# A forward and backward pass in one kernel: the last wq product in one piece, and seven zero stores in other places

## The chip, the cores and the metric

The kernel runs on one core of a Trainium2 chip. The metric is the time of one execution on the device in microseconds, as the median of several runs. A core has engines that run side by side and wait for each other through semaphores: TensorE (PE in the profile, with its weight loads as PEld), VectorE (DVE), ScalarE (ACT), GpSimd (POOL) and SyncE (SP), which here does little but issue transfers (DMAs). Data lies in HBM; the engines work on SBUF (128 partitions), and TensorE writes to PSUM, from where VectorE or ScalarE must copy a result before it can be stored ("eviction").

## The reference

One token goes through four layers that use the same weights: attention (A1), MLP (B2), attention (A3), MLP (B4), each on the layer norm of its input and added to it. Then all gradients are computed.

```
# attention: 32 query heads, 4 key heads, the last W=4096 of 32768 cached positions
q = x @ wq;  p = softmax(q k^T * Dh**-0.5);  out = (p v) @ wo
# MLP: D=1024, F=3584
h = x @ w1 + b1;  act = h * tanh(softplus(h));  out = act @ w2
# forward
x = x + A(layernorm(x)); x = x + B(layernorm(x)); x = x + A(layernorm(x)); x = x + B(layernorm(x))
out, vjp = jax.vjp(f, x, k_cache, v_cache, wq, wo, w1, b1, w2);  return out, *vjp(grad_out)
```

With one token every product is a matrix by a vector, and every weight's gradient is an outer product of two vectors, summed over the two layers that share the weight. The gradients of the key and value caches have the caches' full length: the 28672 positions ahead of the window are zero, and must be stored as zeros, 512 KB at a time in 112 pieces.

## The kernel before

All instructions are written out in the order in which each engine runs them; nothing is reordered. SP's order is thus the order of the calls in the source, and a transfer that stands behind another in it is issued behind it. There are eight semaphore lanes for SP's transfers, so a transfer is issued only when the eighth before it has landed.

**Weights.** wq, K, V and wo are loaded at the start. w1 and w2 do not fit beside them and are streamed through rings of buffers: `queue` lists the loads in order, and `rel(ring, i)`, called when a buffer has been used, lets `pump()` issue the next load into it (lines 157 to 212). A load is therefore issued when an older piece is done with, some pieces ahead of its own use.

**The chain.** Forward: `attn_fwd` A1, `mlp_B2_fwd`, `attn_fwd` A3, `mlp_B4` (B4's forward and backward in one, in four blocks of w1), then `attn_bwd` for A3, `mlp_B2_bwd`, and `attn_bwd` for A1. The two w2 passes (`w2_pass`, line 598) go over 14 pieces ("chunks") of w2: for each, four products with the activations, eight transposes that ScalarE evicts, a multiply-and-reduce on VectorE (`ttr`), and in the next step eight small products that free the buffer (`pairs`). In B2's backward pass a w1 pass follows, with 16 half rows of w1 in the same manner (line 851). Every stage needs the one before it, so a load that comes late delays everything behind it.

**The zero stores.** `zeros(n)` (line 140) issues the next n stores of zeros on SP at the place in the order where it is called. The calls are spread over the chain: `Z_` in `w2_pass` (a map from the chunk to a count, called behind that chunk's `rel`), `ZB4` behind each block of B4, `Z_` in `attn_fwd` and `attn_bwd` (three and more places each), a map in the w1 pass (line 849), and single calls. The source is a zeroed part of SBUF (`zlo`, `zt`, at the end `z8`).

**The gradients of the weights.** During the last `attn_bwd` (A1), `out_step` starts the jobs that form the gradients: step 0 stores eight zeros, steps 1 and 2 turn rows, and steps 3 to 6 run jobs (`run_jobs`). A dW2 job (`pair_half`) is four outer products on TensorE into four PSUM banks and four evictions by VectorE and ScalarE (`ev_out`, which gives each eviction to the engine with the smaller sum of costs so far); every second one issues two stores of 512 KB out of one of seven stage buffers each. The order of the jobs is 14 dW2 jobs, then dW1 jobs alternating with jobs for dK and dV (four stores of 512 KB after every fourth), then four groups of four 512-KB stores of dWo and two 1-MB stores of dWq.

Step 3 is called when dq of A1 is there; then comes the last product with wq (64 matmuls in `attn_bwd`, line 805), which gives the gradient of the input x, a small output that no other stage needs. Between eighths of this product (`h % 4 == 3`) step 4 runs one job. Every second dW2 job has a third argument of 1 in `add`, by which `run_jobs` issues one zero store behind it.

Of the kernel before, what the change touches and what calls it, by code (L numbers as in the profile page):

```python
# [21 lines left out]
def kernel(  # L22
# [283 lines left out]
    gpair = kt([P, 4, TD], BF16, "gpair")  # L306
# [329 lines left out]
    def mlp_B2_fwd(x_col):  # L636
        zeros(4)
        sv, n_bf, g0 = ln_fwd(x_col, "B2")
        hacc = one_tile("acc", TF)
        for i in range(16):  # L640
            t, hf = i // 2, i % 2
            w, ring, sl = take(("w1h", i))
            for b in range(NW2):
                fb = hf * NW2 + b
                o = (b // 2) * 2 * P + b % 2
                mm(hacc[:, fb:fb + 1], w[:, o:o + 2 * P - 1:2], n_bf[:, t:t + 1], i == 0 and b == 0, t == TD - 1)
            rel(ring, sl)
            if i == 1:
                bcast_g(gpair[:, LI["B4"], :])
        zeros(2)  # L650
        h = wk("h", TF)
        nc.vector.tensor_add(h[:], hacc[:], b1_f[:])
        dact = kt([P, TF], FP32, "dact_B2")
        mish(h[:], apair[:, 1, :], dact[:], TF)
        sv["dact"] = dact
        R, dps, ds = w2_pass(apair[:, 1, :], gpair[:, LI["B4"], :], {8: 1, 9: 1, 10: 1, 11: 1})
        nc.gpsimd.memset(sA, 0.0)
        zsrc[:] = [zt, 2048]
        da4 = kt([P, TF], FP32, "da4")
        y = d_cols(R)  # L660
        x_new = kt([P, TD], FP32, "x_B2")
        nc.vector.tensor_add(x_new[:], x_col[:], y[:])
        da_merge(da4[:], dps, ds)
        return x_new, sv, da4
# [84 lines left out]
    def attn_bwd(g_col, g_bf, l, sv, last, nxt, F_, Z_, step):  # L749
        fill_kind("wo")  # L750
        big = two_banks()
        for d in range(TD):
            for n in range(8):
                mm(big[n // 4][32 * (n % 4):32 * (n % 4) + 32, :].rearrange("p (h x) -> p h x", h=4),
                   bc(g_bf[:, d:d + 1]), wo[:, 4 * n:4 * n + 4, d * P:(d + 1) * P], d == 0, d == TD - 1, tile_position=(0, 32 * (n % 4)))
        if last:
            p_t, ds_t = sB, wo[:, 1, :]
            wo_dead()
            nc.gpsimd.dma_start(wo[:, 0, :], p3_d[:])
        else:  # L760
            p_t, ds_t = sv["p"], sA
        zeros(Z_[0])
        acc = one_tile("acc", HQ)
        j_cols(big, acc, 8, F_[0], True)
        do32 = wk("do32", HQ)
        nc.vector.tensor_copy(pad[:, :, 0:8], acc[:].rearrange("p (g h) -> p g h", g=G))
        nc.vector.tensor_copy(do32[:], acc[:])
        pr = jkf[:, 0:P]
        nc.vector.tensor_mul(pr[:].rearrange("p (c h) -> p c h", c=NC), do32[:, None, :].to_broadcast([P, NC, HQ]),
                             sv["o32"][:, None, :].to_broadcast([P, NC, HQ]))  # L770
        nc.gpsimd.tensor_copy(dos[:, LI[l], :], do32[:])
        step(0)
        fill(F_[1])
        fill_kind("V")
        big = two_banks()
        scores(big, Vf, False)
        sps = sm_tile(P, 1)
        mm(sps[:], pr[:], one[:], True, True)
        sd = wk("sd", 1)
        nc.vector.tensor_copy(sd[:], sps[:])  # L780
        zeros(Z_[1])
        for h in range(2):
            nc.vector.scalar_tensor_tensor(out=ds_t[:, h * 512:(h + 1) * 512], in0=big[h][:], scalar=sd[:, 0:1],
                                           in1=p_t[:, h * 512:(h + 1) * 512], op0=ALU.subtract, op1=ALU.mult)
        sv["p"], sv["ds"] = p_t, ds_t
        if not last:
            nc.gpsimd.dma_start(p3_d[:], sB)
            nc.gpsimd.dma_start(sB, p1_d[:])
            sv["p"] = wo[:, 0, :]
        step(1)  # L790
        fill(F_[2])
        to_keys(ds_t)
        fill_kind("K")
        qacc = one_tile("acc", HQ)
        step(2)
        keys_mm(K[:], fold, qacc, F_[3])
        if not last:
            rings["rb"] += [7, 1, 2, 3, 4, 5, 6]
            pump()
        nc.scalar.activation(dqpair[:, LI[l], :], qacc[:], ACT.Copy, scale=scale)  # L800
        zeros(Z_[2])
        step(3)
        fill_kind("wq")
        R = one_tile("R", 512)
        for h in range(HQ):
            for hf in range(2):
                g = 2 * hf + h % 2
                mm(R[32 * g:32 * g + 32, :].rearrange("p (t d) -> p t d", t=4), bc(dqpair[:, LI[l], h:h + 1]),
                   wq[:, 4 * hf:4 * hf + 4, h * P:(h + 1) * P], h < 2, h >= HQ - 2, tile_position=(0, 32 * g))
            if h % 4 == 3 and h < 31:  # L810
                step(4)
        y = d_cols(R, hook=lambda: step(5))
        tt = wk("xx", 2 * TD)
        nc.vector.tensor_copy(tt[:, 0:TD], y[:])
        return ln_bwd(tt, sv, g_col, nxt, hook=lambda: step(6))

    def mlp_B2_bwd(g_col, g_bf, sv, x3):
        bcast_g(g_bf)
        R, dps, ds = w2_pass(apair[:, 0, :], g_bf, {10: 1})
        zeros(3)  # L820
        dh = kt([P, TF], FP32, "dh_B2")
        da_merge(dh[:], dps, ds, sv["dact"][:])
        nc.vector.tensor_copy(hpair[:, 1, :], dh[:])
        y = d_cols(R)
        x4_bf = kt([P, TD], BF16, "x4_bf")
        nc.vector.tensor_add(x4_bf[:], x3[:], y[:])

        NT, NV = 4, 3
        dhb = [kpf, jk[:]]
        for hf in range(2):  # L830
            for v in range(2):
                ncb = 2 if v == 0 else 1
                ps = ptile(FP32, "dhp")
                for i in range(ncb):
                    for tt in range(2):
                        col = hf * NW2 + 2 * (NT + 2 * v + i) + tt
                        mm(ps[:, i * 256 + tt:i * 256 + tt + 255:2], bc(hpair[:, 1, col:col + 1], P), ident_bf[:], i == 0 and tt == 0, True)
                evac(dhb[hf][:, v * 512:v * 512 + ncb * 256], ps[:, 0:ncb * 256], ncb * 256, "DA"[(hf + v) % 2])
        nacc = one_tile("acc", TD)
        nv = wk("nv", 16)  # L840
        pend = []

        def pairs(i, w, ring, sl):
            t, hf = i // 2, i % 2
            for k in range(8):
                fb = hf * NW2 + k
                mm(nacc[:, t:t + 1], w[:, k * P:(k + 1) * P], hpair[:, 1, fb:fb + 1], i == 0 and k == 0, hf == 1 and k == 7)
            rel(ring, sl)
            zeros({9: 2, 12: 1, 14: 1}.get(i, 0))

        for i in range(16):
            w, ring, sl = take(("w1h", i))
            T8([w[:, (k // 2) * 256 + k % 2:(k // 2) * 256 + k % 2 + 255:2] for k in range(8)], w[:, 0:1024], "A")
            ttr(w[:, 1024:1792], dhb[i % 2][:, 0:768], nv[:, i:i + 1])
            if pend:
                pairs(*pend.pop())
            pend.append((i, w, ring, sl))
        pairs(*pend.pop())
        tt = wk("xx", 2 * TD)
        n3 = nv[:].rearrange("p (t h) -> p t h", h=2)  # L860
        t3 = wk("t3", TD)
        nc.vector.tensor_add(t3[:], n3[:, :, 0], n3[:, :, 1])
        nc.vector.tensor_add(tt[:, 0:TD], t3[:], nacc[:])
        sv["dh"] = dh
        return ln_bwd(tt, sv, g_col, "A1"), x4_bf
# [168 lines left out]
    def wo_dead():  # L1034
# [42 lines left out]

        for n in range(NW2 // 2):
            add("w2a", n, lambda c=2 * n: pair_half(row_sp["w2"], c, w2_out, w2_lhs, 0))
            add("w2", n, lambda c=2 * n: pair_half(row_sp["w2"], c, w2_out, w2_lhs, 1), 1)  # L1080
        for n in range(16):
            add("w1", n, lambda t=n // 2, hf=n % 2: w1_job(t, hf))
            add("kv", n, lambda n=n: kv_step(n))
# [26 lines left out]
    def out_step(i):  # L1110
        if i == 0:
            nc.scalar.copy(z8.bitcast(FP32), zlo[:, 0:2].bitcast(FP32).to_broadcast([P, 2048]))
            zsrc[:] = [z8, 4096]
            zeros(8)
        elif i < 3:
            rows_turn(row_sp["w2"], i - 1, w2_sp[i - 1], "rep")
        elif i > 2:
            run_jobs(1 if i == 4 else 2)

    ZB4 = [12, 11, 9, 7]  # L1120
    FT4 = [(0, 0, 0, 0), (10, 2, 2, 2), (10, 2, 2, 2), (10, 2)]
    FB4 = [(1, 0), (1, 0), (1, 0), (1, 2)]

# [3 lines left out]
    x3, sA3 = attn_fwd(x2, "A3", False, sB, [3, 2, 8, 2, 2, 2], [8, 4, 17])  # L1127
    tt, sB4 = mlp_B4(x3, da4)
    g3, g3b, _ = ln_bwd(tt, sB4, gcol, "A3", nfill=2)
    g2, g2b, _ = attn_bwd(g3, g3b, "A3", sA3, False, "B2", [4, 3, 5, 2], [3, 1, 3], lambda i: None)  # L1130
    (g1, g1b, _), x4_bf = mlp_B2_bwd(g2, g2b, sB2, x3)
    zeros(4)
    g0, g0b, _ = attn_bwd(g1, g1b, "A1", sA1, True, "X0", [0] * 4, [0, 0, 0], out_step)
# [39 lines left out]
```

## Time and profile before

| what | value |
|---|---|
| median of 3 runs | 432.07 us (430.75 to 433.14) |
| profiled execution | 431.02 us, span from first to last instruction 429.2 us |
| bytes moved | 170.5 MB (70.8 read, 99.1 written), mean 397 GB/s |
| busy share | PE 75%, VectorE 55%, ScalarE 51%, GpSimd 4% |
| mean granted clock of TensorE | 0.757 |
| zero stores of 512 KB out of `misc` | 97, median 10.2 us from issue to landing |
| eviction in a job, ScalarE / VectorE | 629 / 599 ns |

The busy time of an engine does not tell whether it bounds the kernel: TensorE's matmuls overlap, and a share is an average over stages. The DMA row of the page is near full throughout; the rate beside it in GB/s tells where the transfers queue and where there are gaps. In the lists of instructions, "[0.64 <-DMA K<-in_B_w_dram]" means that the engine sat idle for 0.64 us and that a load into K from a weight of B ended it. The tile names are those of the buffers: loads of w2 and w1 in the backward pass go into K, those of the forward pass into wo and misc; a store "out_dram<-misc" is one of zeros.

### The profile page before, as it was taken

The page shows a single profiled execution, that of the slowest core. Times are in us where ns is not written, and L with a number is a line of the kernel's source. Part 1 is how long each engine was busy: PE and PEld are TensorE (multiplying, and loading weights), DVE is VectorE, ACT ScalarE, POOL GpSimd, SP SyncE. Part 2 cuts the span into 40 slices and gives each one's busy share as a digit, 9 for nine tenths or more (in the row PEclk, how much of TensorE's full clock was granted, in tenths as well). Part 3 has the DMA queues.
Part 4 walks back from the last instruction along what each step waited for, and adds up shares of the span by engine and source line. Part 5 has one row for each costly group of instructions (what it writes and reads, how often), then busy time and mean ns, then how long its engine had stood idle before and what let it go on. Part 6 is the DMA issues. An engine that isn't in the chain of part 4 may idle for free.

```text
span 429.2 us, 9216 instructions
## 1 busy us (share of the span) xinstructions
PE 321.2 (75%) x3732; PEld 188.3 (44%) x3732; DVE 234.4 (55%) x532; ACT 219.1 (51%) x335; POOL 15.4 (4%) x54
## 2 busy tenths in 40 slices
PE   3476736367697898878788898887799799999830
PEld 1154315345455587756646565764423223321100
DVE  2035102068535346555537288673367998899940
ACT  1036101036436356646534267482487699999940
POOL 2000000000000000000000000000400111000000
PEclk9999555569889979999989989685955555555555
DMA  8999999999999999999999999999999999999995
GB/s 329 423 419 419 411 408 399 406 407 378 387 418 409 417 417 365 417 409 384 381 408 406 350 397 386 373 362 421 411 421 417 419 413 413 403 409 412 410 413 242
DMA packets 49975, 170.50 MB, mean 397 GB/s; under 512 B 4848, under 2 KB 5900, under 8 KB 45836
## 3 DMA queue, kind: packets, MB, share of 16 engines
q1 hardware_dynamic: 49456, 168.84, 99.2%
q0 software_dynamic: 416, 1.06, 0.7%
q8 instruction: 29, 0.48, 0.4%
q14 instruction: 14, 0.11, 0.1%
q10 hardware_dynamic: 60, 0.01, 0.0%
HBM read 70.79 MB, written 99.10 MB: 396 GB/s over the span
## 4 chain that ended last, share of the span: by engine, by line
DMA 40%; PE 35%; ACT 11%; DVE 7%; issue 3%; SPq 0%; ACTq 0%; DVEq 0%
DMA K<-in_B_w_dram 9%; DMA wo<-in_A_wo_dram 8%; PE tp L264 8%; PE R L244 7%; DMA out_dram<-misc 7%; DMA K<-in_A_k_cache_dram 5%; DMA wo<-in_B_w_dram 4%; PE sm L244 4%; PE acc L244 4%; ACT wo L899 4%; PE op L244 3%; ACT K L237 3%; PE lo L244 3%; DMA out_dram<-wo 3%; ACT wq L899 3%
## 5 line engine op out<-in xcount | busy, mean ns | idle before, releaser
L237 ACT COPY K<-tp 128x1024 bf16<-128x1024 bf16 x60 | 58.8, 1016 | 14.3 <-PE tp L264 13.3
L264 PE MATMUL tp<-ident_bf,K 128*128 128x128 bf16 x656 | 52.0, 238 | 6.4 <-ACT K L237 2.8
L244 PE MATMUL op<-wo 2*128 2x512 bf16 (+2 forms) x123 | 52.1, 562 | 5.0 <-ACT wo L899 2.7
L244 PEld LDWEIGHTS <-wo 128*128 128x128 bf16 (+2 forms) x590 | 24.4, 101 | 61.8 <-issue 53.5
L264 PEld LDWEIGHTS <-K 128*128 128x128 bf16 x656 | 44.3, 109 | 12.7 <-issue 9.6
L237 ACT COPY wo<-tp 128x1024 bf16<-128x1024 bf16 x33 | 33.5, 1023 | 25.7 <-PE tp L264 22.9
L899 ACT CAST wo<-op 128x512 bf16<-128x512 f32 (+1 forms) x51 | 31.2, 629 | 7.9 <-DMA out_dram<-wo 1.8
L596 DVE CUSTOM_DVE_ANT_0 K<-K,kp 128x1024 bf16<-128x1024 bf16 (+1 forms) x22 | 24.6, 1127 | 2.8 <-PE R L244 1.0
L235 DVE COPY jk<-R 128x512 f32<-128x512 f32 (+1 forms) x11 | 7.3, 665 | 33.9 <-PE R L244 33.9
L264 PE MATMUL tp<-ident_bf,wo 128*128 128x128 bf16 x336 | 24.4, 226 | 0.6 <-ACT wo L237 0.5
L244 PE MATMUL acc<-wo 2*128 2x512 bf16 (+1 forms) x41 | 24.3, 593 | 0.2 <-DVE V L896 0.2
L244 PE MATMUL hi<-wo 2*128 2x512 bf16 x41 | 24.3, 592 | 0.0
L244 PE MATMUL lo<-wo 2*128 2x512 bf16 x41 | 24.1, 587 | 0.0
L264 PEld LDWEIGHTS <-wo 128*128 128x128 bf16 x336 | 20.1, 101 | 6.9 <-issue 6.8
L237 ACT CAST jk<-hi 128x512 bf16<-128x512 f32 x4 | 2.6, 661 | 37.7 <-PE hi L244 37.7
L244 PE MATMUL sm<-wo 2*128 2x512 bf16 (+1 forms) x33 | 19.8, 600 | 1.3 <-DVE cols L384 1.3
L896 DVE CAST wo<-op 128x512 bf16<-128x512 f32 (+1 forms) x32 | 18.4, 599 | 4.1 <-PE tp L930 1.5
L235 DVE CAST jk<-lo 128x512 bf16<-128x512 f32 x4 | 2.8, 711 | 31.9 <-PE lo L244 31.9
L235 DVE COPY K<-tp 128x1024 bf16<-128x1024 bf16 x22 | 14.9, 690 | 9.6 <-PE tp L264 9.5
L244 PE MATMUL R<-wo 2*128 2x512 bf16 (+1 forms) x33 | 19.6, 593 | 0.6 <-DVE wo L896 0.4
L237 ACT COPY wq<-tp 128x1024 bf16<-128x1024 bf16 x13 | 13.0, 1018 | 11.7 <-PE tp L264 8.8
L364 ACT ACTIVATE cols<-cols,eps_t 128x1 f32<-128x1 f32 x4 | 1.2, 294 | 33.4 <-DVE cols L361 33.4
(293 smaller groups left out, 656.2 us busy)
## 6 DMA issues: line engine op xcount, KB each, us to landing
out_dram<-misc SPq DMA_DIRECT2D x97, 512.0 KB, 10.2
out_dram<-wo SPq DMA_DIRECT2D x39, 512.0 KB, 9.4
K<-in_B_w_dram SPq DMA_DIRECT2D x28, 512.0 KB, 8.1
K<-in_A_k_cache_dram SPq DMA_DIRECT2D x9, 1024.0 KB, 14.9
wq<-in_A_wq_dram SPq DMA_DIRECT2D x8, 1024.0 KB, 10.0
out_dram<-wq SPq DMA_DIRECT2D x8, 1024.0 KB, 13.5
K<-in_B_w_dram SPq DMA_DIRECT2D x16, 448.0 KB, 6.1
out_dram<-wo SPq DMA_DIRECT2D x16, 448.0 KB, 7.2
```

Of the source, the lines that this page charges most:

```text
L235: return nc.vector.tensor_copy(out_ap, in_ap)
L237: return nc.scalar.copy(out_ap, in_ap)
L244: return nc.tensor.matmul(out_ap, lhsT=lhsT, rhs=rhs, start=start, stop=stop, skip_group_check=True, **kw)
L264: nc.tensor.transpose(ps[:, b * P:(b + 1) * P], ap, ident_bf[:])
L364: nc.scalar.activation(lnv[:], var[:], ACT.Ln, bias=eps_t[:, 0:1], scale=1.0)
L596: return nc.vector.tensor_tensor_reduce(out=w, in0=w, in1=vec, scale=1.0, scalar=0.0, op0=ALU.mult, op1=ALU.add, accum_out=acc_col)
L896: nc.vector.tensor_copy(out_ap, in_ap)
L899: nc.scalar.copy(out_ap, in_ap)
```

## The change

The product with wq in the last `attn_bwd` is no longer interrupted: step 4 is not called, and the jobs that ran in it follow behind the product, in the same order. dW2's jobs no longer issue zero stores. The seven stores go to other calls: one behind chunk 2 in the w2 pass of B2's forward pass, two behind dq in A3's backward pass (3 becomes 5), one behind chunk 1 and two at the end of the w2 pass of B2's backward pass (3 becomes 5), and one behind step 4 of the w1 pass. In addition one store moves from block 0 of B4 to block 2. The `attn_bwd` of A3 never ran jobs in step 4, so its product is as before.

```diff
 # mlp_B2_fwd
-        R, dps, ds = w2_pass(apair[:, 1, :], gpair[:, LI["B4"], :], {8: 1, 9: 1, 10: 1, 11: 1})
+        R, dps, ds = w2_pass(apair[:, 1, :], gpair[:, LI["B4"], :], {2: 1, 8: 1, 9: 1, 10: 1, 11: 1})
 # attn_bwd, in the loop over heads of the wq product
-            if h % 4 == 3 and h < 31:
-                step(4)
 # mlp_B2_bwd
-        R, dps, ds = w2_pass(apair[:, 0, :], g_bf, {10: 1})
-        zeros(3)
+        R, dps, ds = w2_pass(apair[:, 0, :], g_bf, {1: 1, 10: 1})
+        zeros(5)
 # the w1 pass
-            zeros({9: 2, 12: 1, 14: 1}.get(i, 0))
+            zeros({4: 1, 9: 2, 12: 1, 14: 1}.get(i, 0))
 # the list of jobs
-            add("w2", n, lambda c=2 * n: pair_half(row_sp["w2"], c, w2_out, w2_lhs, 1), 1)
+            add("w2", n, lambda c=2 * n: pair_half(row_sp["w2"], c, w2_out, w2_lhs, 1))
 # out_step
-            run_jobs(1 if i == 4 else 2)
-
-    ZB4 = [12, 11, 9, 7]
+            run_jobs(2)
+
+    ZB4 = [11, 11, 10, 7]
-    g2, g2b, _ = attn_bwd(g3, g3b, "A3", sA3, False, "B2", [4, 3, 5, 2], [3, 1, 3], lambda i: None)
+    g2, g2b, _ = attn_bwd(g3, g3b, "A3", sA3, False, "B2", [4, 3, 5, 2], [3, 1, 5], lambda i: None)
```

## The prediction

> **What bounds the kernel now.** I read the page's slices first, then the windows of 5 us, then the timeline around the loads, then the waits of the store queue. The slices (columns: busy tenths, granted clock, GB/s in 40 slices of 10.7 us):
>
> ```profile
> PEclk9999555569889979999989989685955555555555
> DMA  8999999999999999999999999999999999999995
> GB/s 329 423 419 419 411 408 399 406 407 378 387 418 409 417 417 365 417 409 384 381 408 406 350 397 386 373 362 421 411 421 417 419 413 413 403 409 412 410 413 242
> ```
>
> The DMA row says that transfers are always under way, but the rate says more: 418 GB/s where stores queue (155 to 160 us), and holes to 350. A 512-KB zero store at 418 GB/s costs 0.524 MB / 0.418 = 1.25 us. That is the price of each moved store wherever the transfers queue; in a hole it is free. So the question is which it meets. Windows (columns: engines' busy us and counts, clock, DMA share, GB/s):
>
> ```profile
> 220.00:225.00 5.00, 4.84 (x63) 2.15 (x63) 1.27 (x5) 1.01 (x1) 0.00 (x0) 0.66 1.02 394
> 240.00:245.00 5.00, 4.20 (x73) 2.08 (x70) 0.69 (x1) 1.03 (x2) 0.00 (x0) 1.00 0.92 331
> 275.00:280.00 5.00, 4.10 (x80) 3.23 (x79) 5.00 (x13) 5.00 (x6) 0.00 (x0) 0.98 0.98 343
> 280.00:285.00 5.00, 4.30 (x80) 3.28 (x78) 4.30 (x10) 4.91 (x6) 0.00 (x0) 1.00 0.98 348
> 310.00:315.00 5.00, 4.67 (x40) 1.63 (x40) 3.17 (x5) 3.72 (x8) 0.00 (x0) 0.78 1.02 431
> 315.00:320.00 5.00, 5.00 (x44) 1.40 (x40) 3.13 (x5) 3.65 (x7) 0.00 (x0) 0.50 1.01 418
> 320.00:325.00 5.00, 5.00 (x40) 1.47 (x36) 2.72 (x5) 4.21 (x7) 0.00 (x0) 0.50 1.03 415
> 325.00:330.00 5.00, 4.75 (x29) 2.35 (x25) 3.66 (x6) 3.71 (x7) 0.00 (x0) 0.50 1.03 417
> 330.00:335.00 5.00, 3.26 (x19) 1.25 (x22) 4.57 (x17) 3.13 (x6) 0.00 (x0) 0.50 1.03 419
> 415.00:420.00 5.00, 0.00 (x0) 0.00 (x0) 0.00 (x0) 0.00 (x0) 0.00 (x0) 0.50 1.03 415
> ```
>
> From 310 us the transfers are full; the last eviction ends at 413 and stores drain to 428. Ahead of that, the chain waits for weights that queue behind zero stores:
>
> ```profile
> 188.23 0.40 PE L244 MATMUL lo<-K,npair 128*32 128x512 bf16 x4 [2.84 <-DMA K<-in_B_w_dram]
> ...
> 243.85 2.98 SPq L149 DMA_DIRECT2D out_dram<-misc  x3
> 251.72 9.33 SPq L182 DMA_DIRECT2D K<-in_B_w_dram  x8
> 258.25 0.40 PE L244 MATMUL R<-K,apair 128*32 128x512 bf16 x4 [0.64 <-DMA K<-in_B_w_dram]
> ...
> 276.20 8.08 SPq L182 DMA_DIRECT2D K<-in_B_w_dram  x9
> 286.09 1.04 PE L264 MATMUL tp<-ident_bf,K 128*128 128x128 bf16 x8 [1.18 <-DMA K<-in_B_w_dram]
> ```
>
> And the end is not simply a full queue: between 340 and 381 us SP, which issues the stores, itself waits for evictions (us in total, times, longest):
>
> ```profile
> SPq L1002 <- ACT wo L899: 6.5, 8, 1.2
> SPq L1002 <- DVE wo L896: 3.2, 3, 1.4
> SPq L1002 <- ACT K L899: 2.8, 3, 1.2
> ```
>
> The waits of that stretch sum to 19.5 of 41 us, while the evicting engines wait for a store only once there (0.8 us). So dW1, dK and dV run at the pace of the evictions, and only the last block (dWo and dWq) is bound by transfers: its first store is issued at 381.73 and lands 6.7 us later; 15 more stores of 1.25 us and 8 of 2.5 us are 38.8 us, and the last lands at 428.2, 39.8 us on.
>
> **The change, part by part.** Seven stores, 8.8 us of transfers, leave the dW2 jobs; bytes and instructions stay. A step counts as far as it moves 381.73 (the first dWo store) or the drain behind it.
>
> *One zero in the first w2 pass (after chunk 2).* From 100 to 110 us every chunk's first product starts within 0.05 us of its load's landing, at a pitch of 1.25 us: saturated. The new store stands in SP's queue ahead of chunk 9's load, so chunks 9 to 12 come 1.25 later; chunk 13's load is limited by its own issue (104.75 to 110.4) and gives 0.7 back, until the loads of 160 us, which start right behind a run of zeros, take it up again. Bounds 0 and +1.25; I take +1.1, near the upper end, since the pitch is that of a full queue.
>
> *One zero from B4's block 0 to block 2.* Block 2's loads queue behind block 0's zeros: 8.1 us from issue to landing, where block 1's, behind fewer, took 5.6, and PE idles 2.84 us for them (188.23). One store less gives -1.25 (bounds -1.25 and 0). In block 2 it delays only K loads not needed until 236, and fills the hole of 238 to 244 us (311 GB/s). Taken: -1.25.
>
> *Two zeros behind dq in A3's backward pass, one after chunk 1 of the second w2 pass.* SP issues the two at some 247.7 and 249, ahead of chunk 7's load (251.72, landing at 258.2, 6.5 us). The transfers run at 363 to 418 GB/s in between, 0.4 us short of full, so chunk 7 comes 2.1 to 2.5 later, and it has no slack (0.64 wait above). Chunk 1's store is ahead of chunk 9's load: another 1.25. From chunk 7 on the pitch is 1.28, the transfers' own, and VectorE's 1.15 to 1.23 a chunk wins nothing back. Bounds +2.3 (hole and deeper queue help) and +3.75; taken +3.5.
>
> *Zeros 3 to 5 behind that pass, one after step 4 of the w1 pass.* The hole at 276 to 278 (268 GB/s) holds 0.9 us and step 7 has 0.25 slack, so 2.5 become 1.4. From step 7 the loads set the pace at 1.1 each; step 4's store adds 1.25, but the slow stretch from 280 to 288 (352 GB/s, 1.3 us under full) may take it in. Bounds +1.5 and +3.75; taken +2.2.
>
> Together the chain reaches the last attention's backward pass 5.55 later.
>
> *The product in one piece.* Before, 8 heads' worth ran between jobs. From the first evictions (311.3) to the last dW2 store (336.9) VectorE and ScalarE are idle 6.5 and 5.6 us (25 us less the busy sums of the five rows from 310, 17.25 and 18.42, less the 1.3 and 1.0 ahead of the first), mean 6.0; two waits for stage buffers (329.4 and 333.3, some 1 us each) are in it and go with the seven zeros. After, the first pair's evictions end at 314.2 and the engines sit until the product, begun at 312.4, is through. The nearest row is the product of the same 64 matmuls at 220.72: its first half ran at half clock, the rest at full (0.66 in the row), 5.1 us; the wq product at 240.18 took 3.6 at full clock; all at half would be 16 groups of 0.427 = 6.8. With 5.1 it ends at 317.5, the idle is 3.7, and 1.5 of other waits (the 1.3 that PE waits for the layer norm's columns among them) stay: 5.2, so -0.8; the stage wait of 376 goes too: -1.3 in sum. With 3.6 it is -2.9; with 6.8 and no gain at 376, +1.7.
>
> Here the Trainium skill has a rule: in "TensorE: Matmul & The Clock Gate", Part 1, the half clock is the default and about 3.4 us of busy array lift it. By it an unbroken product would lift the clock where the chopped one did not, the 5.1 case; without it, at 0.5 as in the rows from 315 on, the 6.8 case, which puts the sum 1.7 to 2.5 us higher. The row at 220 agrees with the rule: half clock for 3.4 us, then full.
>
> *The relief of the drain.* With no zeros queued, the first dWo store still stands behind four dK stores that kv's last job releases together at 377.2: an unqueued load takes 4.3 (issue of 276.20), so 377.2 + 4.3 + 4 x 1.25 = 386.5 against 388.4: -2.0 at most. With stores of dW1 still queued, -0.5. Taken -1.8. The 39.8 us behind it do not change: that is why 8.8 us less to store gains 2.
>
> POOL issues the same work; SP issues no more transfers than before, and its order is otherwise kept.
>
> **Sum.** +1.1 -1.25 +3.5 +2.2 -1.3 -1.8 = +2.45 us. The profiled execution took 431.0 (span 429.2 and 1.8 around it), so 433.5; the median of the three runs shown, 432.07, is 1.05 above it, so I predict 434.5. Ends added: -2.35 and +9.95.
>
> **Rivals.**
> (a) *The drain bounds everything from 310 us on.* For it: 409 to 431 GB/s in all rows. Against: SP's 19.5 us of waits for evictions. Were the evictions able to run ahead, the end would move by the chain less all seven stores: +5.55 - 8.75 = -3.2, so 427.8, or 428.9 by the median. It decides where the first dWo store is issued no later than its old place (381) although the chain comes 5.5 later; from 384 on the end is not earlier than before (384 + 4.3 = 388.3).
> (b) *The holes take the stores in.* Losses against 418 GB/s between 245 and 291 us sum to some 4 us; if all are filled, the two backward terms are 3.4 in place of 5.7, and with 0 for the first pass the sum is near -1: 431. Against: the pace there is set by landings.
> (c) *Everything is paid and the product stays at half clock*: +1.25 -1.25 +3.75 +3.3 +1.7 -1 = +7.75: 439.8.
>
> **How the numbers follow.** Forecast (shift of +0.5 to +5) 0.50, (c) 0.20, (b) 0.14, (a) 0.16. About 0.5% (2.2 us) is what a measurement of this kernel can tell. Faster: (a) and a little of (b), 0.18. Same: the rest of (b) and 0.12 of the forecast, 0.24. Slower: 0.58. Range: 429.5 (all but most of (a)) to 440.5 (with (c)); the forecast's own is 432.5 to 437.
>
> **What will show it.** In the profile after: chunk 7 of the second w2 pass some 2.5 us further behind the pass's start and chunk 13 3.5; PE's wait for B4's block 2 shortened to 1.6; step 7 of the w1 pass waiting for its load by over 1 us; the 64 matmuls unbroken and 5 us long; the first dWo store at some 386 and the last landing 45 us behind it. I am wrong if the w2 pass keeps its length, if the rate between 315 and 345 stays at 415 with no hole, or if the drain behind the first dWo store is shorter than 44 us.

## The result, and the profile after

The changed kernel takes 437.19 us (median of 4 runs, 435.93 to 438.11), the kernel before 432.31 us beside it (4 runs, 430.75 to 433.14). The ratio is 1.0099, with a 95% interval of 1.0073 to 1.0125: slower by 4.3 us (3.2 to 5.4), or 4.9 by the medians. The prediction was +2.45.

The profiled execution of the changed kernel took 437.84 us, with a span of 436.1. It is 0.65 us above its median, while the profiled execution of before (431.02) was 1.3 below its own. The two traces thus show 6.9 us between the spans, 2.0 to 2.6 more than the runs do. This matters below.

The three slice rows of the page after:

```profile
PEclk9999555569799889989989895875886555555555
DMA  8999999999999999998999999999998979999997
GB/s 330 424 420 417 411 408 402 408 407 404 406 414 408 417 408 387 387 385 308 369 415 406 396 398 370 359 409 421 408 426 329 368 302 404 386 374 411 408 412 319
```

Two kinds of gap are seen. One is new: slices 30 to 32 (329, 368, 302 GB/s, about 327 to 360 us), where the seven stores no longer stand behind the dW2 jobs. The other lies earlier and is not new: slice 18 (308, 196 to 207 us), deeper than before (384), and slices 24 and 25 (370 and 359, 262 to 284 us), where before had 373 and 362 one slice later. The windows of 5 us of the changed kernel (columns as before: busy us and counts of PE, PEld, DVE, ACT, POOL, then clock, DMA share, GB/s):

```profile
240.00:245.00 5.00, 4.26 (x75) 2.13 (x74) 0.72 (x2) 1.21 (x2) 0.00 (x0) 1.00 1.04 389
...
320.00:325.00 5.00, 4.67 (x48) 2.33 (x52) 1.89 (x3) 2.74 (x6) 0.00 (x0) 0.80 1.01 425
...
330.00:335.00 5.00, 4.32 (x27) 2.72 (x27) 3.68 (x9) 3.00 (x6) 0.00 (x0) 0.50 0.71 287
335.00:340.00 5.00, 4.41 (x26) 1.50 (x24) 4.63 (x13) 5.00 (x10) 0.00 (x0) 0.50 0.70 279
...
350.00:355.00 5.00, 4.54 (x30) 1.49 (x30) 4.53 (x11) 3.50 (x9) 3.00 (x11) 0.50 0.63 242
```

At 330 to 340 us VectorE and ScalarE are busy 60 to 100% of the time while the transfers run at 280 GB/s; 10 us earlier, in the same part of the work, before had 415 and 417. (The window of 240 to 245 us, 331 before, now has 389: more is in flight there, none of it for chunk 7.) In the new gap the evictions set the pace: the store queue waits for them in 27.2 of the 33 us from 327 to 360.

The time is lost ahead of that. This is the timeline around the loads of the second w2 pass, changed kernel (start, duration or stretch, engine, line; in brackets the idle time and what ended it):

```profile
246.81 5.93 SPq L149 DMA_DIRECT2D out_dram<-misc  x5
...
253.32 1.78 SPq L182 DMA_DIRECT2D K<-in_B_w_dram  x2
...
255.76 0.55 SPq L149 DMA_DIRECT2D out_dram<-misc  x1
...
257.24 8.57 SPq L182 DMA_DIRECT2D K<-in_B_w_dram  x5
...
263.64 0.62 PE L244 MATMUL R<-K,apair 128*32 128x512 bf16 x4 [5.70 <-DMA K<-in_B_w_dram]
...
276.50 2.82 SPq L149 DMA_DIRECT2D out_dram<-misc  x5
...
282.74 4.41 SPq L182 DMA_DIRECT2D K<-in_B_w_dram  x5
...
290.40 1.03 PE L264 MATMUL tp<-ident_bf,K 128*128 128x128 bf16 x8 [2.96 <-DMA K<-in_B_w_dram]
```

Five zero stores now stand ahead of chunk 7's load, and TensorE waits 5.70 us for that chunk where it waited 0.64. Five more stand ahead of the w1 pass's step 7, and it waits 2.96. The chain that ended last goes by loads a little behind these two. Its longest pieces in this stretch are the load of chunk 9, issued behind one more zero store (257.24, landed at 267.47); the fourth of the five stores ahead of the w1 pass (278.07); and the load of step 12, issued when that store had landed (288.42):

```profile
257.24 10.23 DMA K<-in_B_w_dram
...
278.07 10.27 DMA out_dram<-misc
...
288.42 8.86 DMA K<-in_B_w_dram
```

29 of the 40 us from 257 to 297 us are loads and a zero store; before had no zero store among the long pieces there. At chunk 7 VectorE is 5.6 us later than before (258.69 to 264.30; 0.7 of it is there when the pass starts), at the last attention's backward pass 10.0 (300.90 to 310.90), and at 380.41 us of before still 9.1.

The wait for chunk 7 has a sequel. These are the windows behind it, first of the changed kernel, then of before:

```profile
265.00:270.00 5.00, 4.60 (x58) 3.18 (x56) 3.12 (x7) 2.84 (x3) 0.00 (x0) 0.50 1.00 385
...
260.00:265.00 5.00, 4.64 (x82) 3.22 (x81) 4.86 (x8) 3.93 (x5) 0.00 (x0) 1.00 0.99 380
```

In the changed kernel TensorE's granted clock is half from 261.55 us for 10.24 us, and the products of chunks 7 to 11 follow each other at 1.7 us (2.2 where chunk 9's load ends a wait of 0.40), against 1.27 at full clock before. The loads of chunks 10 and 11 landed at 268.74 and 269.98, ahead of their products at 269.23 and 270.93, so there TensorE and not the transfers sets the pace. From chunk 7 to chunk 13 this kernel takes 10.0 us, before 7.6.

The product in the timeline of the changed kernel (start, duration):

```profile
322.38 5.32 PE L244 MATMUL R<-wq,dqpair 128*32 128x512 bf16 x64
```

The 64 matmuls run unbroken. The end of the drain, in the DMA issues of the changed kernel: the first dWo store, issued at 390.30, and the last dWq store, issued at 422.00 (size, us from issue to landing):

```profile
out_dram<-wo SPq DMA_DIRECT2D x1, 512.0 KB, 4.4
...
out_dram<-wq SPq DMA_DIRECT2D x1, 1024.0 KB, 13.0
```

The first dWo store is issued 8.6 us later than before (381.73), but lands in 4.4 us instead of 6.7, with little queued ahead of it. The waits of the store queue for evictions from 350 to 391 us add up to 26.9 of 41 us, against 19.5 of 41 from 340 to 381 us of before; the two longest rows (us in total, times, longest):

```profile
SPq L1000 <- DVE wo L894: 12.0, 8, 3.0
SPq L1000 <- ACT wo L897: 5.4, 7, 1.1
```

### The profile page after: what moved, and what is told of

Its sections match the earlier page's. It is cut to its first block, busy times and chain, and to the rows that moved or that the text cites. A ratio compares the mean times of both kernels' runs of the same rounds, so it can differ in the third digit from the quotient of the medians.

```text
span 436.1 us, 9207 instructions
## 1 busy us (share of the span) xinstructions
PE 323.6 (74%) x3732; PEld 192.6 (44%) x3732; DVE 233.7 (54%) x532; ACT 218.3 (50%) x335; POOL 15.4 (4%) x54
## 4 chain that ended last, share of the span: by engine, by line
PE 25%; ACT 10%; DMA 8%; DVE 5%; issue 2%; SPq 0%; ACTq 0%; DVEq 0%
DMA K<-in_B_w_dram 6%; ACT wo L897 5%; PE R L244 5%; PE tp L264 5%; PE op L244 4%; PE acc L244 3%; PE sm L244 3%; ACT wq L897 3%; PE lo L244 2%; DMA out_dram<-misc 2%; PE hi L244 2%; ACT K L237 2%; PE tp L928 1%; DVE wo L894 1%; DVE jk L235 1%
## 5 line engine op out<-in xcount | busy, mean ns | idle before, releaser
L264 PE MATMUL tp<-ident_bf,K 128*128 128x128 bf16 x656 | 55.2, 247 | 8.7 <-DMA K<-in_B_w_dram 3.8
L264 PEld LDWEIGHTS <-K 128*128 128x128 bf16 x656 | 46.8, 113 | 16.0 <-issue 10.6
L244 PE MATMUL hi<-wo 2*128 2x512 bf16 x40 | 23.1, 579 | 0.0
L244 PE MATMUL sm<-wo 2*128 2x512 bf16 (+1 forms) x36 | 21.6, 600 | 0.0
L244 PE MATMUL R<-wo 2*128 2x512 bf16 (+1 forms) x36 | 21.4, 593 | 0.0
L235 DVE COPY wo<-tp 128x1024 bf16<-128x1024 bf16 x19 | 12.8, 689 | 10.2 <-PE tp L264 10.1
L244 PEld LDWEIGHTS <-npair 128*32 128x32 bf16 x184 | 6.2, 116 | 26.0 <-issue 22.6
```

The source lines that it names most:

```text
L235: return nc.vector.tensor_copy(out_ap, in_ap)
L244: return nc.tensor.matmul(out_ap, lhsT=lhsT, rhs=rhs, start=start, stop=stop, skip_group_check=True, **kw)
L264: nc.tensor.transpose(ps[:, b * P:(b + 1) * P], ap, ident_bf[:])
```

## The experiments

Three theories stood after the result. **T1**: the seven stores are paid by the chain, because they queue ahead of loads for which it waits, and the tail gives back only a little. **T2**: the product in one piece, or the gaps in the drain, cost the end. **T3**: the store taken from block 0 of B4 is the surprise. The trace after has 248 GB/s at 200 to 205 us where before had 321, and more transfers are in flight ahead of the second w2 pass, so a queue that ran dry at 202 us would be paid for at 258. Rival (a) of the prediction, the drain as the bound from 310 us on, is tested as well.

Ratios are to runs of the kernel before on the same chip, whose medians were 432.2 to 432.9. One thousandth is 0.43 us, and prices below are ratios times 432.3.

### The product alone

```diff
-            if h % 4 == 3 and h < 31:
-                step(4)
 ...
-            run_jobs(1 if i == 4 else 2)
+            run_jobs(2)
```

> The product alone in one piece, the seven zero stores left in the dW2 jobs. T1 (the seven stores ahead of the loads cost the chain 10 us, the product gives 0.9 back): nothing moves ahead of 310 us, the 64 matmuls take 5.1 to 5.4 us, and the time is 0.5 to 1.5 us under the kernel before (431 by its median of 432.3). T2 (the engines that evict stand still behind the unbroken product, the store queue runs dry, and that costs the end): 2 to 4 us over it, 434.5 to 436.5, with slices under 350 GB/s between 312 and 325 us.

Measured: 432.20 us (12 runs), ratio 0.9989 (0.9971 to 1.0007): -0.5 us, not told apart from nothing. T2 falls for the product. The product takes 5.32 us as in the changed kernel, and in this run, with the seven stores behind the jobs, the transfers never let go. Windows of this kernel:

```profile
325.00:330.00 5.00, 4.41 (x24) 1.39 (x24) 4.48 (x10) 5.00 (x10) 0.00 (x0) 0.50 1.03 419
330.00:335.00 5.00, 3.08 (x19) 0.81 (x18) 4.26 (x12) 4.18 (x9) 0.00 (x0) 0.50 1.03 419
```

Its first dWo store among the DMA issues:

```profile
out_dram<-wo SPq DMA_DIRECT2D x1, 512.0 KB, 6.7
```

The evictions behind the product come up to 5.4 us later than before at 314 us, 2.1 later at 328 and on time at 336; at 380 us they are 0.9 later again. What the pause holds up, the next 20 us make good, and the first dWo store still takes 6.7 us to land.

### The seven stores alone

```diff
-w2_pass(apair[:, 1, :], gpair[:, LI["B4"], :], {8: 1, 9: 1, 10: 1, 11: 1})
+w2_pass(apair[:, 1, :], gpair[:, LI["B4"], :], {2: 1, 8: 1, 9: 1, 10: 1, 11: 1})
 ...
-        R, dps, ds = w2_pass(apair[:, 0, :], g_bf, {10: 1})
-        zeros(3)
+        R, dps, ds = w2_pass(apair[:, 0, :], g_bf, {1: 1, 10: 1})
+        zeros(5)
 ...  (w1 pass, A3's backward pass, ZB4 and the jobs as in the change)
```

> All seven stores moved as in the change (block 0 of B4 to block 2 too), the product still in eighths between the jobs. T1: the chain comes to the last attention's backward pass 10 us later, as in the changed kernel, and the time is that of the changed kernel plus 0.9 lost with the product: 437.5 to 438.5 (5 to 6 over before). T2: the stores cost only what the drain doesn't give back, and without the unbroken product the time is within 2 us of before, 431 to 434.

Measured: 437.54 us (6 runs), ratio 1.0105 (1.0084 to 1.0126): +4.5 us, as T1 had it. That is the whole loss of the change; the product's share in it is -0.3 (1.0099 against 1.0105), less than the runs tell apart. VectorE is 11.4 us later at 300.9 us and 9.9 at 380.

### The seven stores left out, with and without the product in one piece

```diff
         job, f, z = jobs.pop(0)
         f()
-        zeros(z)
+        del zero_jobs[:z]
```

> The product in one piece, and the seven stores of the dW2 jobs left out altogether: 3.7 MB of the zeros of the cache gradients are never written. The chain is that of the kernel before, the tail that of the changed kernel, 10 us earlier. T1: only product (-0.9) and relief (-2.2) are seen: 3.1 us under before, 429. Rival (a), the transfers bound everything from 310 us on: all seven stores are gained, 8.75 us, 423.5. T2: no gain or a loss, 432 to 435.

> The seven stores of the dW2 jobs left out altogether (3.7 MB of the cache gradients' zeros are never written), the product in eighths as before. T1: the relief of the drain alone, 2.2 us under before, 430; the difference to the run with the product in one piece is the product's 0.9. Rival (a): 8.75 us under before, 423.5.

Measured: with the product in one piece 429.15 us, ratio 0.9917 (0.9888 to 0.9945), -3.6 us; with it in eighths 429.95 us, ratio 0.9928 (0.9910 to 0.9947), -3.1 us; T1 had 429 and 430. Rival (a) falls: 8.75 us of transfers vanish and 3.1 us are gained. T2 falls for the gaps as well: they are there (below), and the time is lower. The product is worth another -0.5, again within the interval. What the tail looks like without the seven (product in eighths), in windows:

```profile
325.00:330.00 5.00, 4.75 (x30) 0.81 (x28) 4.04 (x7) 3.96 (x8) 0.00 (x0) 0.50 0.98 399
330.00:335.00 5.00, 4.64 (x24) 2.81 (x24) 4.26 (x13) 3.20 (x7) 0.00 (x0) 0.50 0.79 316
335.00:340.00 5.00, 3.78 (x22) 0.65 (x19) 4.79 (x16) 3.71 (x8) 0.00 (x0) 0.50 0.71 286
...
345.00:350.00 5.00, 4.84 (x27) 1.19 (x26) 4.83 (x11) 5.00 (x12) 0.93 (x6) 0.50 0.78 305
```

And its first dWo store, issued at 381.94, among the DMA issues:

```profile
out_dram<-wo SPq DMA_DIRECT2D x1, 512.0 KB, 4.3
```

The dWo store is issued when it was before (381.73) and lands 2.2 us sooner (386.28 for 388.47). Between 330 and 350 us the transfers have room that no eviction fills.

The run with all seven moved and this one have the same tail, the product in eighths and no store behind a job, and differ in the chain alone. So the seven stores, with the move in B4, cost the chain 1.0105 - 0.9928 = 0.0177, or 7.6 us (+-1.2), for 8.75 us of transfers.

### The move in B4, taken back and alone

```diff
-    ZB4 = [12, 11, 9, 7]
+    ZB4 = [11, 11, 10, 7]
```

> The changed kernel with block 0 and block 2 of B4 left at 12 and 9 zero stores. T1 with the prediction's price of that move (-1.25 in the chain): 438.5, 1.3 over the changed kernel's 437.2. T3 (a store less in block 0 lets the store queue run dry near 202 us, and the bytes not moved there come back ahead of the second w2 pass): the stretch from 200 to 210 us is back at 320 to 370 GB/s, chunk 7 of that pass comes 2.5 to 3 us sooner than in the changed kernel, and the time is 434 to 435.5.

> The kernel before with one zero store moved from block 0 of B4 to block 2, and nothing else. T1 with the prediction's price: -1.25, so 431. T3: 200 to 210 us falls to 250 to 300 GB/s, the loads of the second w2 pass land 2.5 to 3 us later, and the time is 434.5 to 435.5.

Measured: the changed kernel without this move 437.58 us, ratio 1.0106 (1.0072 to 1.0141), as the changed kernel; the move alone 431.95 us, ratio 1.0006 (0.9985 to 1.0027). So it is worth +0.3 us (+-0.9): neither the -1.25 of the prediction nor T3's +2.5 to +3. T3 falls, and the gap that it started from is not the move's doing: the same stretch has 178 GB/s in the run with the seven stores left out, and 174 in the one with the product alone, where nothing was changed ahead of it. The window of the first of these:

```profile
200.00:205.00 5.00, 4.26 (x78) 3.44 (x76) 2.10 (x4) 2.88 (x3) 0.00 (x0) 1.00 0.51 178
```

Why the -1.25 did not come is seen in TensorE's waits for blocks 2 and 3 with the move alone:

```profile
186.41 0.40 PE L244 MATMUL lo<-K,npair 128*32 128x512 bf16 x4
...
187.75 0.40 PE L244 MATMUL lo<-K,npair 128*32 128x512 bf16 x4
...
190.18 0.40 PE L244 MATMUL lo<-K,npair 128*32 128x512 bf16 x4 [1.02 <-DMA K<-in_B_w_dram]
...
191.50 0.40 PE L244 MATMUL lo<-K,npair 128*32 128x512 bf16 x4
...
208.35 0.40 PE L244 MATMUL hi<-K,npair 128*32 128x512 bf16 x4 [1.74 <-DMA K<-in_B_w_dram]
```

Block 2's last product and block 3's wait in the trace of before:

```profile
192.22 0.40 PE L244 MATMUL lo<-K,npair 128*32 128x512 bf16 x4
...
208.96 0.40 PE L244 MATMUL hi<-K,npair 128*32 128x512 bf16 x4 [1.64 <-DMA K<-in_B_w_dram]
```

The first load of block 2 is in time; the wait of 2.84 us is gone. But four loads follow each other, and the third now ends a wait of 1.02: the last product of the block starts 0.7 earlier than before (191.50 for 192.22), though the first starts 1.8 earlier (186.41 for 188.23). Block 3 waits as long as before (1.74 for 1.64), and at 300.9 us the chain is 0.7 later.

### The three stores around the second w2 pass, and the three around the w1 pass

Three of the seven are moved in each and the other four left out (that part of the edit is not shown), so that the tail is that of the run with none.

```diff
-  [4, 3, 5, 2], [3, 1, 3], lambda i: None)        # first kernel
+  [4, 3, 5, 2], [3, 1, 5], lambda i: None)
-  w2_pass(apair[:, 0, :], g_bf, {10: 1})
+  w2_pass(apair[:, 0, :], g_bf, {1: 1, 10: 1})
 ...
-        zeros(3)                                   # second kernel
+        zeros(5)
-            zeros({9: 2, 12: 1, 14: 1}.get(i, 0))
+            zeros({4: 1, 9: 2, 12: 1, 14: 1}.get(i, 0))
```

> The three early stores around the second w2 pass alone (two behind dq, one behind chunk 1); the last four dW2 jobs' stores and the first three are out of the tail, of which the four are never written (2 MB of the cache gradients' zeros). The tail is that of the run with all seven left out, 430.0, so the difference to it is the chain's price of these three. Prediction's term: +3.5, 433.5. If the three themselves cost all that the changed kernel showed there (+6.7): 436.7. If the loads absorb them (rival (b)): under +1, 431.

> The three early stores around the w1 pass alone (zeros 3 to 5 ahead of it, one behind step 4), four of the dW2 jobs' stores never written (2 MB of zeros), so that the tail is that of the run with all seven left out, 430.0. Prediction's term: +2.2, 432.2; sized by the changed kernel's trace: +3, 433; all three paid in full: +3.75, 433.8; rival (b): under +1, 431.

Measured: the second w2 pass 433.49 us, ratio 1.0030 (1.0006 to 1.0054); the w1 pass 432.75 us, ratio 1.0005 (0.9988 to 1.0023). Against the run with none (0.9928) the prices are 4.4 us (+-1.3) and 3.3 us (+-1.1); taken as plain differences of medians, 3.5 and 2.8. The 3.75 us that three stores take lies in both intervals, so that payment in full fits both; for the w1 pass the interval reaches down to 2.2. Rival (b), under 1 us, falls twice. In the timelines, the wait for chunk 7 in the first of the two kernels:

```profile
243.28 5.65 SPq L149 DMA_DIRECT2D out_dram<-misc  x5
...
260.65 0.62 PE L244 MATMUL R<-K,apair 128*32 128x512 bf16 x4 [4.49 <-DMA K<-in_B_w_dram]
```

The wait for the w1 pass's step 7 in the second:

```profile
270.16 3.75 SPq L149 DMA_DIRECT2D out_dram<-misc  x5
...
284.62 1.04 PE L264 MATMUL tp<-ident_bf,K 128*128 128x128 bf16 x8 [2.14 <-DMA K<-in_B_w_dram]
```

VectorE's shift in the first kernel is +2.6 at chunk 7, +4.3 at chunk 10 and +4.2 at 380 us, though this run starts the pass 1.1 us earlier than the trace of before; in the second it is +4.1 at 280.6 and at 380. In the run with none, steps 7 and 8 of the w1 pass wait 0.71 and 0.30 us, so not all of the 2.14 is the stores' doing.

### The store behind chunk 2 of the first w2 pass

```diff
-w2_pass(apair[:, 1, :], gpair[:, LI["B4"], :], {8: 1, 9: 1, 10: 1, 11: 1})
+w2_pass(apair[:, 1, :], gpair[:, LI["B4"], :], {2: 1, 8: 1, 9: 1, 10: 1, 11: 1})
```

> The store behind chunk 2 of the first w2 pass alone; the first dW2 job's store is thereby out of the tail and the other six are never written (3 MB of the cache gradients' zeros), so that the tail is that of the run with all seven left out (430.0, ratio 0.993 to before). Prediction's term: +1.1, ratio 0.9955. If it is what the run with all seven moved leaves after the prices of the others (7.6 - 4.4 - 3.3 - 0.3 = -0.4): no price, ratio 0.992 to 0.993.

Measured, with the other six stores left out: 429.96 us, ratio 0.9935 (0.9909 to 0.9961): 0.3 us over the run with none, +-1.4. The trace of this run has the pass 1.4 us later at its end, that of the changed kernel 0.2 earlier. Between 0 and a full store nothing is settled.

### Two stores where the queue runs dry

If a price depends on the place, the stretch at 200 us should be free. Two kernels keep five stores in the jobs and put two elsewhere, with the product in one piece:

```diff
-    ZB4 = [12, 11, 9, 7]
+    ZB4 = [12, 13, 9, 7]     # second kernel: [12, 12, 9, 7], and {2: 1, 8: 1, ...} in the first w2 pass
-  add("w2", n, lambda c=2 * n: pair_half(row_sp["w2"], c, w2_out, w2_lhs, 1), 1)
+  add("w2", n, lambda c=2 * n: pair_half(row_sp["w2"], c, w2_out, w2_lhs, 1), int(n >= 2))
```

> The product in one piece; two stores moved from the first two dW2 jobs to the end of block 1 of B4 (13 there), five left in the jobs. Theory of places: the stretch from 200 to 208 us, where the queue runs dry ahead of block 3's loads, takes both for 0 to 1 us, and five stores fit in what the evictions leave free from 325 to 350 us (290 of 418 GB/s in the run with none), so most of the 3 us of relief is kept: 429.5 to 431, ratio 0.994 to 0.997. Rival: every early store costs the chain the same 1.1 (7.6 / 7), and five in the tail still hold up the dWo stores: 432 to 434, ratio 1.000 to 1.004.

> As the run before it, with one store behind block 1 of B4 (12 there) and one behind chunk 2 of the first w2 pass. Theory of places: one store in the hole for 0 to 0.5, the other for 0 to 1.1: 429.5 to 431, ratio 0.994 to 0.997. Rival: 1.1 for each, 432 to 434, ratio 1.000 to 1.004. If it is over the run with both behind block 1 by 1 us, the store behind chunk 2 is paid in full.

Measured: 433.37 us, ratio 1.0030 (1.0002 to 1.0058), and 433.53 us, ratio 1.0013 (0.9987 to 1.0039). Neither beats the kernel before; against the product alone they are +1.8 (+-1.4) and +1.0 (+-1.4). The theory of places falls, and the trace of the first suggests both halves of the reason. Block 3's wait in its timeline:

```profile
212.49 0.62 PE L244 MATMUL hi<-K,npair 128*32 128x512 bf16 x4 [3.56 <-DMA K<-in_B_w_dram]
```

Its first dWo store among the DMA issues:

```profile
out_dram<-wo SPq DMA_DIRECT2D x1, 512.0 KB, 6.1
```

The gap at 200 us was no room: two loads for which TensorE waited 1.64 us in the trace of before are issued into it (there at 202 and 203 us, here at 203.6 and 204.5), and whatever is in flight then delays them. The two stores lengthen that wait to 3.56, and VectorE's shift goes from +1.6 at 191 us to +4.2 at 210. In the second kernel, with one store there, block 3's loads end waits of 1.41 and 0.99 and the shift does not grow (+3.2 at 191, +3.1 at 210), so this half of the reason rests on one trace. And with five stores in the tail the first dWo store still takes 6.1 us to land, against 6.7 with seven and 4.3 with none.

### The early stores at a quarter of their size

```diff
+    def small(n):
+        for _ in range(n):
+            zf, i = zero_jobs.pop(0)
+            src = zlo[:, 0:512] if zsrc[1] == 1024 else zsrc[0][:, 0:512]
+            nc.sync.dma_start(zf[:, i * 2048:i * 2048 + 512], src)
 ...  (called for the seven stores at the places of the change)
```

> The changed kernel with the seven early stores at their places, each of 128 KB in place of 512 KB: three quarters of these seven pieces of the cache gradients' zeros (2.6 MB) are never written. It parts two readings of the 7.6 us that the seven cost the chain. Price by bytes (each store holds up the loads behind it for as long as it takes the 16 DMA engines): a quarter of the price stays, 1.9 us, and the time is 431 to 432.5, ratio 0.996 to 1.001. Price by place (one more entry in SP's queue ahead of the loads, of whatever size): the full price, 437, ratio 1.010.

Measured: 429.63 us (12 runs), ratio 0.9937 (0.9913 to 0.9961). That is 1.4 us under the lower end of the expectation by bytes and 7 under the one by place. Its neighbour is the run with the product in one piece and the seven left out (0.9917): the seven small stores, with the move in B4, cost the chain 0.9 us (+-1.6, which takes in both the 1.9 of a quarter of the price and nothing), where the large ones, by the changed kernel's 1.0099, cost 7.9. An entry in SP's queue alone does not cost the price; that it falls in proportion to the bytes fits, but is not resolved. The profiled execution of this kernel was the slowest of its twelve (432.98), so its trace is not read here.

## Why the prediction was right or wrong

The direction, the place and the mechanism held: the changed kernel is slower, because zero stores ahead of loads are paid by the chain, while 8.8 us less in the tail give back about 3. The size was short by 1.8 us (2.45 against 4.3), and the time of 437.19 lies just above the likeliest case's own range (432.5 to 437). Luck had a part: the chain's four terms were taken as +5.55, and the seven stores cost 7.6 there; a relief of the drain that was larger than its bounds took 1.3 of that back. Term by term, in us:

| term of the sum | predicted | measured |
|---|---|---|
| one store behind chunk 2 | +1.1 | +0.3 (+-1.4) |
| one store from block 0 of B4 to block 2 | -1.25 | +0.3 (+-0.9) |
| three around the second w2 pass | +3.5 | +4.4 (+-1.3) |
| three around the w1 pass | +2.2 | +3.3 (+-1.1) |
| product in one piece | -1.3 | -0.5 (+-0.8) |
| relief of the drain | -1.8 | -3.1 (+-0.8) |
| sum | +2.45 | +4.7; the change itself +4.3 |

**The move in B4** is the term that failed clearly. The prediction took -1.25, the end of its bounds, from one wait of 2.84 us for the first of four loads. The wait went as foreseen, but the third load then ended a wait of 1.02, and block 3's wait remained. The two waits for block 2 in the changed kernel, 1.47 and 0.97, say the same: one wait of 1.6 was forecast. The right value was the other end, 0. This one number is as large as most of the gap.

**The w1 pass** was probably taken too small. The prediction let the hole at 276 to 278 us and the slow stretch to 288 us absorb 1.55 of three stores' 3.75. The price is 3.3, with 2.2 at the lower end of its interval, so that less was absorbed, if anything: step 7 waits 2.96 us in the changed kernel for a load that stands behind five zeros. The predicted sign, a wait over 1 us at step 7, is there.

**The second w2 pass** was right in size, within the interval, and partly in another way. Counted from the pass's first product, as the forecast had it, the changed kernel has chunk 7 4.7 us later than before and chunk 13 7.2; the run with these three alone has 3.5 and 6.2 (forecast 2.5 and 3.5). Not all of that is their price: the run with none of the seven, in which nothing ahead is changed, has 1.4 and 3.1, and the product alone 0.0 and 0.1. What the working lacked is the clock. It let the pass run on at 1.28 us a chunk behind chunk 7, and took chunk 13's further delay from chunk 1's store alone. In all four kernels with these stores at full size the wait for chunk 7 (4.5 to 5.7 us) is followed by 10.24 us at half clock; the run with none has 6.8 us of it too, behind a wait of 1.45, and the one with none and the product in one piece has none there, behind 1.26. No timed run parts the clock's share from the queue's.

**The product** took 5.32 us, forecast 5.1. The granted clock says why. In the changed kernel it is half speed from 322.99 for 3.41 us, then full at 326.40, and half again from 329.8 to the end; so the matmuls took between 379 and 634 ns each. The Trainium skill's rule ("TensorE: Matmul & The Clock Gate", Part 1: some 3.4 us of sustained work lift the half clock) fits the 3.41 us. What a shorter product is worth at the end was over-estimated. With the seven stores still in the tail, evictions delayed by up to 5.4 us are on time again at 336 us, so evictions that come earlier are not likely to gain much there either; without them the traces of the two runs differ by -1.1 between 301 and 380 us (+1.66 to +0.47 against +0.84 to +0.73), near the -1.3. In the runs' times it is -0.5, and no comparison here resolves it.

**The relief of the drain** was right in mechanism: an unqueued first dWo store lands in 4.3 us and at 386.28 us in the run with none of the seven, where the working had 386.5. In the times the relief is larger, 3.1, beyond the end given (-2.0). Of the 39.8 us behind its landing, forecast as unchanged, the changed kernel has 40.2 (394.75 to 434.98). In its tail the first dWo store is issued at 390.3 instead of some 386, for the chain's sake, and the last landing is 44.7 us behind the issue (forecast 45).

**The rivals.** (a) would need 8.75 us from the seven stores; 3.1 came. (b) needed the holes to take six backward stores for 3.4; they cost 7.7. (c), everything paid, came closest: its chain adds up to +7.05, where 7.6 (+-1.2) was measured, but its half-clock product and its small relief did not come. By the prediction's own working a product of 6.8 us leaves 5.4 + 1.5 = 6.9 us of idle time where before had 6.0, which is +0.9 and not the +1.7 that (c) and the upper end of the sum use. And between two jobs four heads ran (8 matmuls), not eight. The forecast's sum uses neither figure.

## What to carry to other kernels

A store put into the queue ahead of loads that the chain waits for costs about its bytes over the rate, here 7.6 us for 8.75 us of transfers, and a low rate in a window is no sign of room: it may be the time in which the loads that count are on their way. A wait in the profile bounds what its removal can gain; look at the next loads behind the one that waited before counting it. One trace against one other can be off by 2 us at a place in the chain, so price a term by timed runs with and without it, with all the rest the same.

## What the runs showed of the hardware that was not expected

A long wait of TensorE for a load is followed by slower work. Behind the wait of 5.70 us for chunk 7 the granted clock was half for 10.24 us, and the chunks came 1.7 us apart in place of 1.27, though two of the loads had landed in time. The same 10.24 us stand behind the waits of 4.5 to 4.8 us in three other kernels; of two waits of 1.45 and 1.26 us, half clock followed one.

Executions of unchanged stretches differ more than the end times do. Four kernels with the same instructions up to 300 us (before, the product alone, and the two with the seven stores left out) have 321, 174, 173 and 178 GB/s from 200 to 205 us, and VectorE stands at 191 us up to 1.75 us later than in the trace of before. The medians of the kernel before stayed within 432.2 to 432.9.

The price of an early store goes with its size: seven stores of 128 KB in place of 512 KB left 0.9 of 7.9 us (+-1.6). And, by one trace each, five stores hold the drain up nearly as long as seven (6.1 and 6.7 us for the first dWo store, 4.3 with none), so that taking two of them away buys little while it is paid in the chain at once. Why the last five count so much was not taken apart.
